# Second product of a feed-forward block in three 256-column matmuls, with its weights rounded at new homes

## The chip, the cores and the metric

The kernel runs on one NeuronCore of a Trainium2 chip. The metric is the time of one execution on the device in microseconds (us), as the median of several runs.

## What is computed

Attention through packed queries, a top-1 mixture of experts, and a feed-forward block follow each other. The change lies almost wholly in the last, `_moe2_ref`. The tensors that matter there are x [4608, 512], w_in [512, 2048] and w_out [2048, 512].

```python
def reference(**kwargs):
    ...
    attn_out = _attn_ref(**attn_kwargs)
    B, H, S, D = attn_out.shape
    x = np.ascontiguousarray(attn_out.transpose(0, 2, 1, 3)).reshape(B * S, H * D)
    x = _moe_ref(x=x, **moe_kwargs)
    return _moe2_ref(x=x, **moe2_kwargs)

def _moe2_ref(x, w_in, w_out) -> np.ndarray:
    h = x @ w_in
    g = h * (1.0 / (1.0 + np.exp(-h)))
    return (g @ w_out).astype(np.float32)
```

## The kernel before

The program has four stages: attention, experts, the feed-forward block's first product (x times W_in, with the activation) and its second (times W_out). Every float32 operand of TensorE is held as two parts: a high part, rounded by ScalarE (`ACT.copy` into an fp32r tile), and a low part, the rest, subtracted by VectorE. A product of two numbers is high x high, high x low and low x high. `tt` (line 849) is the helper behind every addition and subtraction of the feed-forward block, on VectorE or GpSimd, so its line stands in nearly all their rows.

Both products use a scheme of seven block products in place of eight: operands are cut in four quarters (A11, A12, A21, A22 and B11 to B22), sums and differences of quarters are made (S1 to S4, T1 to T4), and the table `terms` pairs them as products 1 to 7. Their results are combined when they are drained from PSUM.

**First product.** It runs in groups `group(z, g)`: z is a sweep over tokens (z = 0 to 3 hold 512 columns, z = 4 holds 256), g one of eight slices of W_in. One group has seven products `Pm`, each of six matmuls; the seventh (`last`) is issued behind the first product of the group after it. `order` is the list of groups behind the eight of z=0; its index is called i, and group 28 in what follows is the group with i = 28. Side work (rounding operands, loading) is queued with `later` and issued by `hook` in four places of a group, as far as a budget of nanoseconds reaches; `flush` issues all that is left. The results are stored in DRAM as c_d[z][0..4]: c11, c12, c21, c22, and for all z but 0 the sum E1 in [4] and a difference in place of c21. z=1 and z=3 share the operand tile X0; z=4 uses tiles `e` (both halves of `sums.ab`). W_in slices sit in four tiles TT[0..3] and are reloaded from t_d with `t_load`.

**Second product.** It runs over 18 units (four per z, two for z=4), each with seven products in `order3`, 126 in all. `split(s)` makes the high and low parts of product s in one of four slots (1024 columns each), `product(s)` runs over the eight slices of W_out, `drain(s)` takes PSUM out, `load_unit` loads the four quarters of a unit (512 KB each) from c_d, and `early_sums` either loads E1 or, where it was not stored, makes it. For each slice there are two matmuls: the high part against 512 columns (high and low W_out side by side), and the low part against 256, summed into the second half of the same PSUM bank:

```python
PE.matmul(out=o, lhsT=h[:, g], rhs=x, start=first and g == 0, stop=False, skip_group_check=True)
PE.matmul(out=o[:, 256:512], lhsT=l[:, g], rhs=x[:, 0:256], start=False, stop=g == 5, skip_group_check=True)
```

So each PSUM result is two half sums of 256 columns. Drains take 512 columns, and GpSimd adds the halves (`both`) before a write to the output.

**W_out.** Its slices are rounded while the first product runs. T1 to T4 of W_out are made in the expert stage by GpSimd (`conv`) and stored in u_d. Slices 5 to 7 go through `corner_steps` into small tiles, from there to v_d in DRAM, and come back with `slice_load` into TT[1..3]. Slice 0 gets homes of its own. Slices 1 to 4 are loaded in seven pieces of four slices into staging tiles (`staged`) and rounded into X0 (`build4`), four pieces at the end of the first product and three beside the first products of the second.

**Order and queues.** Each engine runs its instructions in program order, and the DMAs that an engine issues start in that order too, each behind its waits. Nearly all DMAs are issued by SyncE (SP).

## Time and profile before

| What | Value |
| --- | --- |
| Median of 3 runs | 1289.51 us (1285.29 to 1294.49) |
| The profiled execution, its own time | 1287.26 us |
| Its span, first to last instruction | 1285.4 us |
| Mean granted TensorE clock | 0.985 of full speed |
| TensorE busy | 1201.5 us, 93% |
| VectorE, ScalarE, GpSimd busy | 68%, 42%, 17% |
| First product of the feed-forward block | about 530 to 899 us |
| Second product | 899 to 1285 us |

Busy time is the union of an engine's instructions. Matmuls overlap in the pipeline, so the pace of TensorE is read from the distance between starts and not from the length of one. A time in brackets behind a row is how long the engine sat idle before it, with the one that released it. PEclk is the mean clock that TensorE was granted in a stretch, as a share of 2.4 GHz.

### The profile page before, as it was taken

The numbers are of one execution on the slowest core, as the hardware profiler recorded it, in microseconds if no ns is written. First come the engines' busy times: TensorE is split into PE (matmuls) and PEld (weight loads), VectorE is DVE, ScalarE is ACT, GpSimd is POOL, SyncE is SP. The second block draws the span as 40 slices with busy tenths as digits, with TensorE's granted clock in tenths as the row PEclk, the third lists the DMA queues.
The fourth block names the chain that finished last, engine by engine and source line by source line (L and its number), as shares of the span: only waits on it lengthen the run. The fifth ranks groups of instructions, "written<-read, shape, count | busy, mean of one in ns | idle before, by whom it ended". The sixth has DMA issues, their size and how long they took to land.

```text
span 1285.4 us, 23420 instructions
## 1 busy us (share of the span) xinstructions
PE 1201.5 (93%) x9008; PEld 1040.1 (81%) x9009; DVE 878.3 (68%) x1468; ACT 534.9 (42%) x901; POOL 214.1 (17%) x273
## 2 busy tenths in 40 slices
PE   6898989999999989999999999997878999999998
PEld 4677678999999989878788878776767888888886
DVE  2566657688887784786756667556756777767765
ACT  3666652332243224464444445334423433443342
POOL 3233210113212230100000000000112322323322
PEclk9999999999999999999999999999988999999999
DMA  6898738679877864675864554998744466475561
GB/s 193 247 264 223 238 100 295 218 234 334 275 257 265 279 215 139 201 228 207 335 224 174 193 171 160 377 364 268 239 119 132 125 173 172 132 189 145 151 186 44
DMA packets 260454, 272.67 MB, mean 212 GB/s; under 512 B 35305, under 2 KB 203497, under 8 KB 259057
## 3 DMA queue, kind: packets, MB, share of 16 engines
q1 hardware_dynamic: 253808, 266.40, 65.3%
q10 hardware_dynamic: 6528, 4.72, 1.2%
q8 instruction: 72, 1.18, 0.4%
q14 instruction: 46, 0.37, 0.1%
HBM read 171.59 MB, written 99.48 MB: 211 GB/s over the span
## 4 chain that ended last, share of the span: by engine, by line
PE 44%; DVE 8%; DMA 6%; issue 3%; ACT 2%; SPq 0%; DVEq 0%; POOLq 0%; POOL 0%; ACTq 0%
PE p L1129 17%; PE p L1130 8%; PE p L856 5%; PE p L858 5%; PE p L857 5%; DVE x L849 4%; DMA c_d<-x 1%; DMA x<-u_d 1%; DMA v_d<-e 1%; DVE raw L849 1%; DVE e L849 1%; PE ps L605 1%; PE ps L603 1%; PE ps L604 1%; DMA raww1c<-c_d 1%
## 5 line engine op out<-in xcount | busy, mean ns | idle before, releaser
L849 POOL TENSOR_TENSOR raw<-x 128x256 f32<-128x256 f32 x72 | 100.9, 1402 | 650.1 <-DMA rawe<-c_d 387.9
L849 DVE TENSOR_TENSOR x<-p,x 128x512 f32<-128x512 f32 (+1 forms) x170 | 109.4, 653 | 52.3 <-PE p L858 41.6
L889 ACT ACTIVATE x<-x 128x512 f32<-128x512 f32 (+1 forms) x113 | 67.3, 600 | 131.4 <-DVE x L849 126.2
L1129 PE MATMUL p<-x,e 128*128 128x512 f32 x315 | 118.2, 402 | 0.0
L605 PE MATMUL ps<-hkm,w2s 128*128 128x288 f32 x384 | 113.7, 296 | 2.8 <-DVE w2s L576 2.8
L603 PE MATMUL ps<-hkm,w2s 128*128 128x288 f32 x384 | 114.6, 298 | 1.3 <-DVE yb L614 1.3
L604 PE MATMUL ps<-hqm,w2s 128*128 128x288 f32 x320 | 94.2, 294 | 0.0
L1130 PE MATMUL p<-x,x 128*128 128x256 f32 x320 | 90.4, 282 | 0.0
L603 PEld LDWEIGHTS ps<-hkm,w2s 128*128 128x128 f32 x384 | 72.1, 188 | 7.7 <-DVE hqm L538 3.4
L605 PEld LDWEIGHTS ps<-hkm,w2s 128*128 128x128 f32 x384 | 72.0, 188 | 4.0 <-DVE w2s L576 4.0
L849 DVE TENSOR_TENSOR x<-p,y 128x512 f32<-128x512 f32 (+1 forms) x75 | 49.6, 662 | 36.9 <-PE p L858 26.2
L529 PE MATMUL ps<-at,mh 128*128 128x288 f32 x224 | 66.9, 299 | 7.0 <-PEq L694 4.5
L1129 PEld LDWEIGHTS p<-x,e 128*128 128x128 f32 x315 | 59.9, 190 | 14.9
L531 PE MATMUL ps<-at,mh 128*128 128x288 f32 x224 | 66.9, 298 | 0.0
L530 PE MATMUL ps<-at,mh 128*128 128x288 f32 x224 | 66.8, 298 | 0.0
L534 ACT ACTIVATE hkm<-ps 128x576 fp32r<-128x576 f32 x42 | 27.1, 650 | 85.8 <-PE ps L531 85.8
L575 ACT CAST w2s<-w2c 128x1024 fp32r<-128x1024 f32 x32 | 33.7, 1054 | 67.2 <-PE ps L604 36.6
L1130 PEld LDWEIGHTS p<-x,x 128*128 128x128 f32 x320 | 61.0, 191 | 0.0
L1129 PE MATMUL p<-x,x 128*128 128x512 f32 x160 | 60.5, 404 | 0.0
L604 PEld LDWEIGHTS ps<-hqm,w2s 128*128 128x128 f32 x320 | 60.0, 188 | 0.0
L1129 PE MATMUL p<-x,at 128*128 128x512 f32 x155 | 58.6, 405 | 0.0
L604 PE MATMUL ps<-hvm,w2s 128*128 128x288 f32 x192 | 56.6, 295 | 0.0
(409 smaller groups left out, 3547.4 us busy)
## 6 DMA issues: line engine op xcount, KB each, us to landing
c_d<-x SPq DMA_DIRECT2D x152, 256.0 KB, 2.4
raww1c<-c_d SPq DMA_DIRECT2D x36, 512.0 KB, 7.0
rawe<-c_d SPq DMA_DIRECT2D x36, 512.0 KB, 6.9
w1c<-in_moe_w_dram SPq DMA_DIRECT2D x32, 512.0 KB, 6.5
w2c<-in_moe_w_dram SPq DMA_DIRECT2D x32, 512.0 KB, 6.2
y_d<-yb SPq DMA_DIRECT2D x36, 288.0 KB, 4.8
raw<-y_d SPq DMA_DIRECT2D x36, 256.0 KB, 4.6
vm<-in_v_dram SPq DMA_DIRECT2D x8, 1024.0 KB, 10.7
```

The source lines that it names most:

```text
L529: PE.matmul(out=a[:, i, 0:H2], lhsT=mh[0][:, t, f], rhs=at[0][:, t, n], start=t == 0, stop=False)
L530: PE.matmul(out=a[:, i, 0:H2], lhsT=mh[0][:, t, f], rhs=at[1][:, t, n], start=False, stop=False)
L531: PE.matmul(out=a[:, i, 0:H2], lhsT=mh[1][:, t, f], rhs=at[0][:, t, n], start=False, stop=t == 1)
L603: PE.matmul(out=a[:, i, 0:H2], lhsT=h[:, k, :], rhs=hT(0, k, n), start=k == 0, stop=False)
L604: PE.matmul(out=a[:, i, 0:H2], lhsT=h[:, k, :], rhs=hT(1, k, n), start=False, stop=False)
L605: PE.matmul(out=a[:, i, 0:H2], lhsT=l[:, k, :], rhs=hT(0, k, n), start=False, stop=k == 7)
L849: eng.tensor_tensor(out=o, in0=x, in1=y, op=op)
L856: PE.matmul(out=o, lhsT=h, rhs=a[0][k][:, 0:n], start=start and k == 0, stop=False, skip_group_check=True)
L857: PE.matmul(out=o, lhsT=h, rhs=a[1][k][:, 0:n], start=False, stop=False, skip_group_check=True)
L889: ACT.activation(out=y, in_=x, func=ACTF.Silu)
L1129: PE.matmul(out=o, lhsT=h[:, g], rhs=x, start=first and g == 0, stop=False, skip_group_check=True)
L1130: PE.matmul(out=o[:, 256:512], lhsT=l[:, g], rhs=x[:, 0:256], start=False, stop=g == 5, skip_group_check=True)
```

## The change

The second product uses three matmuls of 256 columns per slice, all into one half bank: high x high, high x low, low x high. The half sums and GpSimd's additions go, and drains take 256 columns. A split is issued behind the drain two products before it, no longer ahead of it. W_out's T1 to T4 are made by VectorE in the feed-forward block (`out_sums`), stored in u_d (`u_store`) for six slices and used at once for slices 0 and 5. Slices 1 to 4 are loaded raw into X0 by GpSimd's queue (`x_load`) once the z=3 sweep is over, into the place of their own low parts, and rounded there (`x_build`). Slices 6 and 7 are loaded and rounded in TT[2] and TT[3] in the same way (`t_raw`, `t_build`); v_d goes. `t_load` moves to GpSimd's queue. The four products that begin unit 0 run over six slices first, and over slices 6 and 7 later. The first sweep's groups from i = 16 on stand in another order: four z=4 groups (28 to 31) now end it. Units run z = 1, 2, 0, 3, 4, and E1 is stored for z=1 and z=2 only (`FIVE`); for the others VectorE makes it in the second product.

```diff
-        if 7 < i < 16 or i >= 24:
+        if 7 < i < 16:
...
-                SP.dma_start(out=u_d[i - 8 if i < 16 else i - 16][:, 512 * n:512 * n + 512], in_=four[n])
+                SP.dma_start(out=u_d[i - 8][:, 512 * n:512 * n + 512], in_=four[n])
...
+    FIVE = (1, 2)
...
-                if not z:
+                if z not in FIVE:
                     store(2, c21)
                     return lambda: None
...
     def t_load(g, x):
         held[g] = x
-        SP.dma_start(out=TT[x][:, 0:3584].bitcast(F32), in_=t_d[g].bitcast(F32))
+        POOL.dma_start(out=TT[x][:, 0:3584].bitcast(F32), in_=t_d[g].bitcast(F32))
...
     def o_load(g):
-        o, p = room(), room()
-        SP.dma_start(out=o[:, 0:256], in_=w[16 + g, :, 0:256])
-        SP.dma_start(out=p, in_=w[24 + g])
-        x4_load(8 + g)
-        ow[g] = o, p
+        ow[g] = raw(w[16 + g]), raw(w[24 + g])
+
+    def out_sums(g, t=None):
+
+        o, p = ow[g]
+        b11, b12, b21, b22 = o[:, 0:256], o[:, 256:512], p[:, 0:256], p[:, 256:512]
+        t1, t2, t3, t4 = t or (b11, b22, b12, b21)
+        return [(425, lambda q=q, x=x, y=y: tt(DVE, q, x, y, ALU.subtract)) for q, x, y in ((t1, b12, b11), (t3, b22, b12), (t2, b22, t1), (t4, b21, t2))]
+
+    def u_store(g):
+        o, p = ow[g]
+        for n, x in enumerate((o[:, 0:256], p[:, 256:512], o[:, 256:512], p[:, 0:256])):
+            SP.dma_start(out=u_d[8 + g][:, 256 * n:256 * n + 256], in_=x)
...
-    units = [(z, r) for z in range(NP2) for r in range(4)] + [(NP2, r) for r in range(2)]
+    units = [(z, r) for z in (1, 2, 0, 3) for r in range(4)] + [(NP2, r) for r in range(2)]
...
     order3 = (1, 7, 6, 2, 5, 3, 4)
+    order0 = (1, 7, 6, 3, 2, 5, 4)
...
     def begin(i):
         if i == 0:
-            slots.append((half(b, 3), one.tile([128, 1024], F32R, name="x6", tag="x6")))
+            x = one.tile([128, 2048], F32R, name="x5", tag="x5")
+            slots.append((half(x, 0), half(x, 1)))
         else:
-            x = one.tile([128, 2048], F32R, name="x5", tag="x5")
-            slots.extend([(half(x, 0), half(x, 1)), (half(b, 0), half(b, 1)), at])
+            slots.extend([(half(X2, 0), half(X2, 1)), (half(b, 0), half(b, 1)), (half(X2, 2), half(b, 2))])
...
     def split(s):
         u, i = seq[s]
         c11, c12, c21, c22 = raws[u % 2]
-        src = {1: c11, 7: c21, 6: c11, 2: c12, 5: E1, 3: c12, 4: c22}[i]
-        h, l = slots[s % R]
-        ACT.copy(out=h, in_=src)
-        tt(DVE, l, src, h.bitcast(F32), ALU.subtract)
-        if i == 1:
-            tt(DVE, c11, E1, c11, ALU.subtract)
-        elif i == 2:
-            tt(DVE, c12, c12, c11, ALU.subtract)
-        elif i == 5 and 0 < u < len(units) - 1:
-            early_sums(u + 1)
+        src = {1: c11, 7: c21, 6: c11, 2: c12, 5: E1, 3: S4, 4: c22}[i]
+
+        def hi():
+            ACT.copy(out=slots[s % R][0], in_=src)
+
+        def lo():
+            h, l = slots[s % R]
+            tt(DVE, l, src, h.bitcast(F32), ALU.subtract)
+            if i == 1:
+                tt(DVE, c11, E1, c11, ALU.subtract)
+            elif i == 6:
+                tt(DVE, S4, c12, c11, ALU.subtract)
+            elif i == 5 and u < len(units) - 1:
+                early_sums(u + 1)
+        return hi, lo
 
     def early_sums(u):
-        if units[u][0]:
+        if units[u][0] in FIVE:
             load_unit(u, (4,))
             return
         c11, c12, c21, c22 = raws[u % 2]
         tt(DVE, E1, c21, c22)
         tt(DVE, c21, c11, c21, ALU.subtract)
...
-    def product(s, gs=(0, 1, 2, 3, 4, 6, 7, 5)):
+    def product(s, gs, start=True, stop=True):
         u, i = seq[s]
         w = terms[i][1]
         h, l = [eight(x) for x in slots[s % R]]
-        o = banks[u % 2][{1: 0, 2: 0, 6: 1, 5: 1, 7: 2, 4: 2, 3: 3}[i]]
-        first = i in (1, 6, 7, 3)
+        o = banks[u % 2][{1: 0, 2: 0, 6: 1, 5: 1, 7: 2, 4: 2, 3: 3}[i]][:, 0:256]
+        first = start and i in (1, 6, 7, 3)
         for g in gs:
             x = WO[g][w]
-            PE.matmul(out=o, lhsT=h[:, g], rhs=x, start=first and g == 0, stop=False, skip_group_check=True)
-            PE.matmul(out=o[:, 256:512], lhsT=l[:, g], rhs=x[:, 0:256], start=False, stop=g == 5, skip_group_check=True)
-
-    tn = [0]
+            PE.matmul(out=o, lhsT=h[:, g], rhs=x[:, 0:256], start=first and g == gs[0], stop=False, skip_group_check=True)
+            PE.matmul(out=o, lhsT=h[:, g], rhs=x[:, 256:512], start=False, stop=False, skip_group_check=True)
+            PE.matmul(out=o, lhsT=l[:, g], rhs=x[:, 0:256], start=False, stop=stop and g == gs[-1], skip_group_check=True)
...
+        a, b, c, d = [x[:, 0:256] for x in banks[u % 2]]
+        n = slice(0, 256)
         if i == 1:
-            ACT.copy(out=p1, in_=a)
-            outs[u] = {}
+            ACT.copy(out=p1[:, n], in_=a)
+            outs[u] = [room(), room()]
         elif i == 6:
-            tt(DVE, u2, b, p1)
+            tt(DVE, u2[:, n], b, p1[:, n])
         elif i == 2:
-            x = t()
-            ACT.copy(out=x, in_=a)
-            outs[u][0] = room()
-            both(outs[u][0][:, 0:256], x)
+            ACT.copy(out=outs[u][0][:, 0:256], in_=a)
         elif i == 5:
-            x = t()
-            tt(DVE, v, b, p1)
-            tt(DVE, x, c, v)
-            outs[u][1] = room()
-            both(outs[u][1][:, 256:512], x)
-        elif i == 3:
-            x = t()
-            tt(DVE, x, d, v)
-            both(outs[u][0][:, 256:512], x)
+            tt(DVE, v[:, n], b, p1[:, n])
+            tt(DVE, outs[u][1][:, 256:512], c, v[:, n])
+        if i == (3 if u else 5):
+            tt(DVE, outs[u][0][:, 256:512], d, v[:, n])
             write(z, r, 0, outs[u][0])
-        elif i == 4:
-            x = t()
-            tt(DVE, x, c, u2)
-            both(outs[u][1][:, 0:256], x)
+        if i == 4:
+            tt(DVE, outs[u][1][:, 0:256], c, u2[:, n])
             write(z, r, 1, outs[u][1])
...
-    def build4(x, src, eng, cast=None):
...
+    def put(d, src, w=None):
+
+        return (lambda: ACT.copy(out=d[:, :, 0:256], in_=src),
+                lambda: tt(DVE, d[:, :, 256:512], src, d[:, :, 0:256].bitcast(F32), ALU.subtract))
+
+    ahead = []
+
+    def chain(*pairs):
+
+        def f(hi, lo):
+            if hi:
+                hi()
+            if ahead:
+                ahead.pop()()
+            if lo:
+                ahead.append(lo)
+        return [(1230, lambda hi=hi, lo=lo: f(hi, lo)) for hi, lo in pairs]
...
+    def corner(g, place):
...
+        return chain(*[put(two(d), x) for d, x in zip(place, src)], (None, None))
+
+    place0 = (mh[1][:, 1024:1536], mh[0][:, 0:1024], mh[0][:, 1024:2048], mh[1][:, 0:1024])
+    place5 = (mh[1][:, 1536:2048], at[0], at[1], half(b, 3))
+
+    def x_load(x):
         i = 512 * names.index(x)
-        put(XX[:, :, i:i + 256], XX[:, :, i + 256:i + 512], src.bitcast(F32).rearrange("p (g n) -> p g n", g=4), eng, cast)
...
-    def staged(x, src):
-        SP.dma_start(out=src.rearrange("p (g n) -> p g n", g=4).bitcast(F32), in_=w_out(x, slice(1, 5)))
-        stage[x] = src
...
-    def slice_load(n, part=None):
-        for a, b in {None: ((0, 3584),), 0: ((0, 512), (2560, 3072)), 1: ((2048, 2560), (512, 1024)), 2: ((1024, 2048), (3072, 3584))}[part]:
-            SP.dma_start(out=TT[1 + n][:, a:b].bitcast(F32), in_=v_d[n][:, a:b].bitcast(F32))
...
+        POOL.dma_start(out=XX[:, :, i + 256:i + 512].bitcast(F32), in_=w_out(x, slice(1, 5)))
+
+    def x_build(x):
+        i = 512 * names.index(x)
+        d = XX[:, :, i:i + 512]
+        return put(d, d[:, :, 256:512].bitcast(F32))
+
+    def t_raw(g):
+        t = two(TT[g - 4])[:, :, 256:512].bitcast(F32)
+        SP.dma_start(out=t[:, 0], in_=w[16 + g, :, 0:256])
+        SP.dma_start(out=t[:, 1:3], in_=w[24 + g].rearrange("p (i n) -> p i n", n=256))
+        SP.dma_start(out=t[:, 3:7], in_=u_d[8 + g].rearrange("p (i n) -> p i n", n=256))
+
+    def t_build(g, a, b):
+        d = two(TT[g - 4])[:, a:b]
+        return put(d, d[:, :, 256:512].bitcast(F32))
...
-    next_t = {19: (4, 0), 20: (5, 1), 23: (6, 2), 24: (7, 3)}
-    b4 = lambda x: (1230, lambda: build4(x, stage[x], DVE))
+    order = [(1, 4), (1, 5), (1, 6), (1, 7), (2, 4), (2, 5), (2, 6), (2, 7), (1, 0), (1, 1), (1, 2), (1, 3), (2, 0), (2, 1), (2, 2), (2, 3),
+             (3, 0), (3, 1), (3, 2), (4, 0), (4, 1), (4, 2), (3, 3), (4, 3), (3, 4), (3, 5), (3, 6), (3, 7), (4, 4), (4, 6), (4, 7), (4, 5)]
+    need = {(2, 4): 2, (3, 0): 3, (4, 0): 4}
+    next_t = {19: (4, 0), 20: (5, 1), 21: (6, 2), 23: (7, 3)}
+    wsum = {8: 1, 9: 2, 19: 3, 21: 4, 22: 6, 24: 7, 25: 0, 26: 5}
+    order2 = ("B11", "T3", "T2", "B22", "B21", "T1", "T4")
...
-        if i in (19, 21, 23, 25):
-            n = (i - 19) // 2
+        if i in wsum:
+            x = wsum[i]
+            o_load(x)
+            if x in (0, 5):
+                later(now + 4, *out_sums(x, tmp), *corner(x, place5 if x else place0))
+            else:
+                later(now + 4, *out_sums(x), (0, lambda x=x: u_store(x)))
+        if i == 28:
             flush()
...
-            for x, y in (("B11", at[0]), ("T3", at[1]), ("T2", half(b, 3)), ("B21", x4)):
-                staged(x, y)
-        if i == 28:
+            load_unit(0, (4,))
+            later(now + 1, (0, small))
+        if i == 29:
+            for x in order2:
+                x_load(x)
+        if i == 30:
             raws[0] = quarters("w1c")
             load_unit(0)
-        if i == 29:
-            later(now + 1, (0, small))
-            later(now + 1, b4("B11"), b4("B21"), b4("T3"))
-        if i == 30:
-            later(now, (0, lambda: slice_load(1)))
-            later(now, b4("T2"), (0, lambda: early_sums(0)), (0, lambda: split(0)))
+            later(now + 1, *chain(*[x_build(x) for x in order2[0:3]]))
         if i == 31:
-            later(now + 1, (0, lambda: slice_load(2)), (0, lambda: begin(1)), (0, lambda: split(1)))
+            t_raw(6)
+            later(now, *chain(*[x_build(x) for x in order2[3:5]], split(0), *[x_build(x) for x in order2[5:7]], (None, None)))
         group(z, g)
         if i - 1 in next_t:
             t_load(*next_t[i - 1])
 
+    S4 = one.tile([128, 1024], F32, name="x6", tag="x6")
     flush()
...
-    pend.pop()()()()
-    slice_load(0, 0)
-    slice_load(0, 1)
...
-    last = {"T1": (1, co[0]), "B22": (2, co[1]), "T4": (3, [half(b, 2)[:, 0:512], half(b, 2)[:, 512:1024]])}
...
+    pend.pop()()()
     raws[1] = quarters("e0")
+    begin(1)
+    t_raw(7)
+    load_unit(1)
+    early = (0, 5, 1, 2, 3, 4)
+    product(0, early, True, False)
+    for s in range(1, R):
+        for f in (*chain(split(s), t_build(6, 2 * s - 1, 2 * s + 1)), *(chain((None, None)) if s == R - 1 else ())):
+            f[1]()
+        product(s, early, True, False)
+    for f in chain(t_build(6, 0, 1), *[t_build(7, a, a + 2) for a in (1, 3, 5)], t_build(7, 0, 1), (None, None)):
+        f[1]()
     for s in range(len(seq)):
         u, i = seq[s]
-        if i == (1 if u else 6) and u + 1 < len(units):
+        if u and i == 1 and u + 1 < len(units):
             load_unit(u + 1)
-        if s == 5:
-            early_sums(1)
-        if s + L < len(seq):
-            split(s + L)
-        for x, (n, t) in last.items():
-            if n == s:
-                for j in range(2):
-                    o = 512 * names.index(x)
-                    d = XX[:, 2 * j:2 * j + 2, o:o + 512]
-                    put(d[:, :, 0:256], d[:, :, 256:512], two(t[j]).bitcast(F32), DVE)
-        if s < 2:
-            product(s, (0, 1, 2, 3, 4, 6, 7))
-            if s:
-                for x in range(2):
-                    product(x, (5,))
-                    drain(x)
+        if s < R:
+            product(s, (6, 7), False)
         else:
-            product(s)
-            drain(s)
+            product(s, range(G))
+        drain(s)
+        if R <= s + L < len(seq):
+            for f in split(s + L):
+                f()
```

## Rows read from the trace of the kernel before

**Rows 1.** Page, busy time: engine, us (share of span), instructions.

```profile
PE 1201.5 (93%) x9008; PEld 1040.1 (81%) x9009; DVE 878.3 (68%) x1468; ACT 534.9 (42%) x901; POOL 214.1 (17%) x273
```

**Rows 2.** Table by stretches: length, busy (instructions) of each engine, PEclk, DMA share, GB/s.

```profile
835.00:860.00 25.00, 23.16 (x124) 19.62 (x123) 12.92 (x26) 8.36 (x18) 0.00 (x0) 1.00 1.01 373
882.00:899.00 17.00, 11.13 (x73) 10.52 (x74) 11.97 (x19) 6.33 (x13) 0.00 (x0) 0.90 0.62 202
930.00:945.00 15.00, 7.56 (x44) 6.33 (x42) 7.98 (x8) 4.84 (x6) 1.97 (x2) 0.81 0.63 176
945.00:972.00 27.00, 22.77 (x114) 19.46 (x115) 17.55 (x17) 8.11 (x9) 6.59 (x4) 0.88 0.35 97
```

**Rows 3.** TensorE's waits, 882 to 980: total us, times, longest.

```profile
PE p L1129 <- DVE y L849: 11.7, 2, 7.4
PE p L856 <- DVE raw L849: 4.4, 2, 4.0
PE p L1129 <- DMA t<-v_d: 3.5, 1, 3.5
```

**Rows 4.** TensorE's waits, 787 to 882.

```profile
PE p L856 <- DVE y L849: 4.5, 3, 1.7
PE p L856 <- ACT y L928: 3.0, 1, 3.0
```

**Rows 5.** TensorE's timeline, first matmuls of products: start, us, line, tiles, size.

```profile
898.88 0.39 PE L1129 MATMUL p<-mh,e 128*128 128x512 f32 x1
...
909.85 0.39 PE L1129 MATMUL p<-mh,e 128*128 128x512 f32 x1
...
912.63 0.39 PE L1129 MATMUL p<-mh,at 128*128 128x512 f32 x1
...
955.60 0.40 PE L1129 MATMUL p<-mh,e 128*128 128x512 f32 x1
...
1002.18 0.40 PE L1129 MATMUL p<-mh,e 128*128 128x512 f32 x1
...
1273.54 0.40 PE L1129 MATMUL p<-mh,e 128*128 128x512 f32 x1
```

**Rows 6.** TensorE's timeline in a z=4 group, ten steps apart.

```profile
850.15 0.28 PE L857 MATMUL p<-e,ta 128*128 128x256 f32 x1
...
851.35 0.28 PE L858 MATMUL p<-e,ta 128*128 128x256 f32 x1
```

**Rows 7.** Page, costliest groups: weight loads; busy us, mean ns of one.

```profile
L1130 PEld LDWEIGHTS p<-x,x 128*128 128x128 f32 x320 | 61.0, 191 | 0.0
```

**Rows 8.** VectorE's timeline: a drain, an early sum, a low part.

```profile
885.01 0.42 DVE L849 TENSOR_TENSOR x<-x,y 128x256 f32<-128x256 f32 x1
...
967.66 1.22 DVE L849 TENSOR_TENSOR x<-rawe 128x1024 f32<-128x1024 f32 x1 [3.85 <-DMA rawe<-c_d]
...
968.92 1.63 DVE L849 TENSOR_TENSOR rawe<-rawe 128x1024 f32<-128x1024 f32 x1
...
970.48 0.68 DVE L849 TENSOR_TENSOR y<-p,y 128x512 f32<-128x512 f32 x1
...
1105.71 1.23 DVE L849 TENSOR_TENSOR e<-rawe,e 128x1024 fp32r<-128x1024 f32 x1 [2.28 <-ACT e L1104]
```

**Rows 9.** VectorE's and GpSimd's timelines at the end.

```profile
1279.46 0.69 DVE L849 TENSOR_TENSOR x<-p,y 128x512 f32<-128x512 f32 x1 [2.12 <-PE p L1130]
...
1280.23 0.72 POOL L849 TENSOR_TENSOR raw<-x 128x256 f32<-128x256 f32 x1 [2.07 <-DVE x L849]
```

**Rows 10.** SyncE's timeline: output writes, a unit's loads.

```profile
956.80 2.07 SPq L1175 DMA_DIRECT2D out_dram<-raw  x2
959.00 4.65 SPq L1077 DMA_DIRECT2D rawe<-c_d  x4
```

**Rows 11.** ScalarE's timeline: a copy of 256 columns, a cast of 1024.

```profile
881.90 0.35 ACT L928 COPY y<-p 128x256 f32<-128x256 f32 x1
...
1104.62 1.05 ACT L1104 CAST e<-rawe 128x1024 fp32r<-128x1024 f32 x1
```

More of the change, by code (lines that the diff above doesn't have):

```diff
@@ L210, in build @@
         with ExitStack() as s1:
-            ffn(tc, s1, sums, y_d, wf_d, t_d, c_d, u_d, v_d, out)
+            ffn(tc, s1, sums, y_d, wf_d, t_d, c_d, u_d, out)
 class Early:
@@ L819, in experts, with ffn @@
                 conv_store(x)
-def ffn(tc, st, sums, y_d, wf_d, t_d, c_d, u_d, v_d, out):
+def ffn(tc, st, sums, y_d, wf_d, t_d, c_d, u_d, out):
     nc = tc.nc
@@ L1210, in ffn @@
     cut = lambda x, o: x[:, o:o + 512]
-    two = lambda x: x.rearrange("p (i n) -> p i n", i=2)
+    two = lambda x: x.rearrange("p (i n) -> p i n", n=512)
     names = ("B11", "B21", "B22", "T1", "T2", "T3", "T4")
     WO = [{x: cut(mh[i // 4], 512 * (i % 4)) for i, x in enumerate(("B21", "B22", "T1", "T2", "T3", "T4", "B11"))}]
-    WO += [{m: cut(x, 512 * i) for i, m in enumerate(names)} for x in (*[X0[:, 3584 * i:3584 * i + 3584] for i in range(4)], *TT[1:])]
+    WO += [{m: cut(X0, 3584 * g + 512 * i) for i, m in enumerate(names)} for g in range(4)]
@@ L1215, in ffn @@
+    five5 = [cut(mh[1], 1536), cut(at[0], 0), cut(at[0], 512), cut(at[1], 0), cut(at[1], 512), cut(half(b, 3), 0), cut(half(b, 3), 512)]
+    WO += [dict(zip(names, five5))]
+    WO += [{m: cut(x, 512 * i) for i, m in enumerate(names)} for x in TT[2:]]
     XX = X0.rearrange("p (g n) -> p g n", g=4)
-    order2 = ("B11", "T3", "T2", "B21", "T1", "B22", "T4")
-    def corner_steps(g, place, eng=DVE):
-        o, p = ow.pop(g)
-        def f(i, src):
-            d, done = place(i)
-            if i:
-                put(two(d)[:, :, 0:256], two(d)[:, :, 256:512], two(src), eng)
-            else:
-                put(d[:, 0:256], d[:, 256:512], src, eng)
-            if done:
-                done(d)
-        return [(1500 if i else 800, lambda i=i, x=x: f(i, x)) for i, x in enumerate((o[:, 0:256], p, x4[:, 0:512], x4[:, 512:1024]))]
@@ L1231, in slice0 @@
-    def slice0(i):
-        return ((mh[1][:, 1024:1536], mh[0][:, 0:1024], mh[0][:, 1024:2048], mh[1][:, 0:1024])[i], None)
-    ring = [*at, half(b, 3)]
-    def slices(n):
-        def place(i):
-            t = ring.pop(0)
-            ring.append(t)
-            a, b = ((0, 512), (512, 1536), (1536, 2560), (2560, 3584))[i]
-            return t[:, 0:b - a], lambda d: SP.dma_start(out=v_d[n][:, a:b].bitcast(F32), in_=d.bitcast(F32))
-        return place
-    def build4(x, src, eng, cast=None):
-        i = 512 * names.index(x)
-        put(XX[:, :, i:i + 256], XX[:, :, i + 256:i + 512], src.bitcast(F32).rearrange("p (g n) -> p g n", g=4), eng, cast)
```

34 lines of the change are left out of this document (7 added, 27 removed).

## The prediction

> **What bounds the kernel now.** I read the page first, for the share of each engine: TensorE is busy 1201.5 us of a span of 1285.4 [rows 1], so time can only come from its idle stretches, from its clock, or from its pace. Then the table by stretches: from 882 to 899 TensorE works 11.1 of 17 us at a mean granted clock of 0.90; from 930 to 945 it works 7.6 of 15; from 945 to 972 its clock averages 0.88 [rows 2]. This is the passage from the first product of the feed-forward part to the second, and the list of waits names what ended the idle time: a VectorE drain of the second product (11.7 us in two waits, the longer 7.4), a VectorE operation of the last z=4 groups (4.4), a load of v_d (3.5) [rows 3]. The stretch before it, 787 to 882, has shorter waits of the same kind between groups of z=4 [rows 4].
>
> The start times of products then size it. Product to product in the quiet stretch is (1273.54 - 1002.18)/96 = 2.827 us; nothing there waits. At that pace the 126 products need 356.2 us. They run from 898.88 to 1273.54 + 2 x 2.827 = 1279.19, which is 380.3: **24.1 us lost**, all of it in units 0 and 1 [rows 5]. The z=4 groups from 882 lose 17 - 11.1 = 5.9 us of idle time and about 17 x 0.10 = 1.7 us of clock, 7.6 together [rows 2]. So the passage costs 31.7 us over a full TensorE, and the groups before it 4.5 + 3.0 = 7.5 [rows 4]. These 39 us are what the reordering can win; the rest of the span is TensorE's pace.
>
> **The change part by part. Three matmuls of 256 columns** (for one of 512 and one of 256) stream the same 768 columns, at 2.4 GHz 320 ns. A pair takes 2.827/8 = 353.3 ns. The nearest row for the new form is a z=4 group, also 256 columns with a weight load each: ten steps from 850.15 to 851.35, 120.0 ns each [rows 6]. Three make 360.0, so 6.7 ns more per slice, x 8 x 126 = **+6.7 us**. Lower bound: pairs ran at (912.63 - 909.85)/8 = 347.5 in one product [rows 5], and triples like that would give -5.9 us. Upper bound: the overhead of a steady pair, (353.3 - 320)/2 = 16.7 ns per matmul, paid three times, is 370 ns, +16.8 us. I take the row of the same form.
>
> A rule speaks against this part. The rows show weight loads hidden: a load lasts 0.19 us [rows 7] and the matmuls that have one each still start every 0.12. The Trainium skill (TensorE: Matmul & The Clock Gate, Part 3, The mechanism) says a weight load overlaps running matmuls only when it targets another row group. Full 128-row weights would then never overlap, and the third load per slice, at the page's 107 ns, would be an estimated 108 us. Here the trace disagrees with it.
>
> **No half sums.** The 72 additions on GpSimd go, and VectorE's drains shrink from 0.69 to 0.42 us [rows 8]. Both are hidden under TensorE in the quiet stretch, where VectorE is not late. They show at the end of the program: the last drain is 0.69 us and the GpSimd addition ends 0.80 us after it [rows 9]; now it is 0.42 and the write follows at once: 0.27 + 0.80 = **-1.1 us**. VectorE gains besides: a 1024-column subtraction beside GpSimd took 1.63 us, alone 1.22 [rows 8].
>
> **The passage.** Count from the start of group 28, the first of the last four z=4 groups. At full pace a z=4 group is 42 x 0.12 = 5.04 us, so four and the last product of the previous sweep end near 21, and the first four products of unit 0 would end at 21 + 4 x 2.88 = 32.5. What can be late:
> - The loads into X0 start when the last z=3 product has read it, near 2.1. They are 3.67 MB, with unit 0's E1 and the stores of c_d some 5.2 MB; at the 373 GB/s that a full stretch moved [rows 2] that is 14 us, the last near 17, B11 near 6. The builds start in group 30, near 12, in load order, so they are covered by 4 to 6 us. GpSimd's queue, which issues them and the t_d loads, has no other work there. Its issue cost no row shows: between nothing and 3 us per load the cover holds; past that each microsecond per load costs up to 5.
> - SyncE loses these issues, and four loads held it 4.65 us [rows 10]. By the Trainium skill (DMA: Bandwidth & Descriptors, Issuing engines are not separate DMA queues) the other queue buys issue time and no bandwidth; on this reckoning the 14 us stand either way. Unit 0's four quarters go out behind the stores of group 29, near 12, and land between 18 and 26; queued behind them are the stores of group 30 and T6's raw slices (near 28), and behind group 31's last store T7's (near 32).
> - VectorE is late next. From 12 it has seven builds and the low part and difference of the first operand, 9 x 1.22, the low part of the second, 1.22, and some nine drains x 0.42: 16 us, so the second product starts near 28, while the first six slices of product 0 end at 22 + 6 x 0.36 = 24. Then T6 pieces, the S4 difference and two low parts put product 3 near 35 to 37, the builds of T7 end near 38.4, four products of two slices take 4 x 0.72, and the fifth waits about 1 us for its operand, split behind the drain of the third: 42.4 against 32.5, **10 us lost**. Cold clock after the gaps of 3 us is in it, as part of the waiting.
> - The four groups themselves: 28 and 29 carry no builds and one sum and one difference less than before; I give them and 30, 31 3 us.
>
> So 13 us in place of 31.7, **-18.7**. Bounds: -28 (the splits and builds all covered but for the last drain) and 0 (the same queueing as now, with T7 as the late load).
>
> **The groups before.** v_d's writes go, z=3 and z=4 lose a sum, a difference and a store per group, while eight slices add four differences of 0.42 each on VectorE (13.4 us over eight groups; VectorE was busy 12.9 of 25 us there [rows 2]). Corner work stays for two slices of four. I let half of the 7.5 remain: **-3.7**, bounds -7 and +4 (three z=4 groups now stand in a row). In the expert stage 32 GpSimd differences and 16 stores go, beside a TensorE that is full: 0, bounds -1 and 0.
>
> **The quiet stretch.** Two things can be late. (a) Units of z=0, 3 and 4 now come from u=8 on, and ten times VectorE makes E1 and c21 itself, when the next unit's quarters have landed. Today that sum waited: load issued at 959.00, sum at 967.66, 8.7 us [rows 8, 10], because the load stood behind the writes at 956.80, which wait for GpSimd; and behind the sum stood the drain (970.48) that the next product needed. Counted from the unit's start at 955.60 [rows 5] the sum came at +12.1. After the change the write is ready at +0.8 to 1.1, takes 1.04, and the third quarter lands near 2.1 + 8.7 = 10.8 to 11.7; the drain stands ahead of the sum. Then 2 x 1.22 and the next low part 1.22 end at 14.4 to 15.3, against 14.4 + 0.24 when product 3 wants it. That is 0 to 0.7 us x 10: **+3**, bounds 0 and +10. (b) A split is now issued after the drain of the product two before it. For products 1 and 2 ScalarE copies (0.35), casts (1.05) [rows 11], VectorE subtracts (1.23) [rows 8]; with 0.2 from product end to the copy that is 2.83 against 2.88 + 0.24: covered by 0.3. If the handovers are half a microsecond longer, 36 x 0.2 = +7; I take 0.
>
> **Sum** against the profiled run's own 1287.3 (span 1285.4, 1.9 around it; the median of the three runs is 1289.5): 6.7 - 1.1 - 18.7 - 3.7 + 3 = -13.8, **1273.5 us**.
>
> **The rivals.** (1) *The passage is limited by its transfers and in-order queues as before.* ScalarE and VectorE take X0's builds, unit 0 and T7 in order, and one late load holds all behind it. For it: the waits of rows 3 are all of this kind, and my reckoning has T7 late already. Against: v_d's 11 MB of writes and reads leave the same stretch. With 13 us more lost: 1286. (2) *Nearly all of the passage is covered,* the builds running into the z=4 groups and the products of six slices bridging the rest: 9 us better, 1264. Against it stands VectorE's 16 us. (3) *The early sums stall the quiet stretch: slower.* If the third quarter lands at +15 instead of +11, VectorE stands still in each of ten units, and each costs what the second of the two drain waits did: 11.7 - 7.4 = 4.3 us, and by the clock of 0.88 over the 27 us that hold both some 1.6 each [rows 2, 3]. That is 10 x 6 = 60 in place of the 3 of the sum: 1331. It decides from a landing later than +11; the order of drain and sum and the earlier write speak against it. (4) *The third weight load shows in full:* up to 1008 x 0.19 = 190 us [rows 7], 1465; the steps of 0.12 in [rows 6] against it. It is what the page's rule above would do here. (5) *It does not do what it says,* the passage keeping its waits for another reason, is the end of (1), 1292.
>
> **How the numbers follow.** Forecast 0.50 (own range 1263 to 1283), (1) with (5) 0.24, (2) 0.17, (3) 0.07, (4) 0.02. The range takes the forecast's bounds, all of (1) and half of (2), and leaves out (3), (4) and the better half of (2): 1258 to 1292. One per cent, about what a measurement of this kernel can tell from no change, is below 1276.6. Faster: 0.33 of the forecast's 0.50, all of (2), 0.04 of (1): 0.54, and I round to 0.56; slower, (3), (4) and a little of (1): 0.10; the rest 0.34.
>
> **What would show it.** In the profile after: three matmuls per slice at 0.120 us and products at 2.88 us (2.78 to 2.96 would be my bounds); no GpSimd additions there; the first product of unit 0 near the end of group 31 with a gap of about 3 us behind its first six slices, then one before T7's slices; no wait longer than 1 us after u=1, with short ones on VectorE's low part of product 3 from u=7 on. Wrong would be: waits on X0's loads (GpSimd's issue), waits in each unit from u=7 on (rival 3), or a product pace beyond 2.96.

## The result, and the profile after

The changed kernel runs in **1268.41 us** (median of four runs, 1267.54 to 1269.88) against 1287.82 for the kernel before on the same chip: a ratio of 0.9843, 95% interval 0.9802 to 0.9883. The forecast was 1273.5, in a range from 1258 to 1292 that holds the measured time. Run once more, beside experiments 5 to 7, the changed kernel gave 1267.28 (0.9842). Its profiled execution took 1268.04, with a span of 1265.6, 19.8 less than before.

The page of the changed kernel answers to [rows 1]: TensorE does the same work in a shorter span, and GpSimd has lost 122 us.

```profile
PE 1202.6 (95%) x10016; PEld 1090.8 (86%) x10017; DVE 853.7 (67%) x1477; ACT 522.4 (41%) x898; POOL 92.6 (7%) x180
```

The table by stretches of the changed kernel, for [rows 2] (length, busy us of PE, PEld, DVE, ACT, POOL, then PEclk, DMA share, GB/s):

```profile
804.00:820.00 16.00, 8.49 (x32) 6.65 (x31) 3.64 (x9) 1.90 (x4) 0.53 (x1) 0.81 0.98 385
820.00:870.00 50.00, 50.00 (x254) 42.68 (x254) 28.33 (x54) 20.09 (x38) 5.39 (x8) 0.99 0.63 218
870.00:882.00 12.00, 12.00 (x102) 12.00 (x101) 6.98 (x15) 6.63 (x14) 0.37 (x1) 1.00 1.02 333
882.00:890.00 8.00, 5.89 (x42) 5.28 (x41) 7.33 (x10) 5.65 (x10) 0.00 (x0) 0.94 0.97 264
890.00:900.00 10.00, 6.94 (x36) 6.54 (x36) 8.03 (x10) 5.46 (x8) 0.00 (x0) 0.71 1.04 325
900.00:920.00 20.00, 18.09 (x147) 17.51 (x146) 13.31 (x18) 8.55 (x14) 0.00 (x0) 1.00 0.54 155
920.00:1000.00 80.00, 80.00 (x669) 80.00 (x668) 49.90 (x56) 29.51 (x36) 0.00 (x0) 1.00 0.57 157
1000.00:1260.00 260.00, 260.00 (x2169) 260.00 (x2169) 184.84 (x199) 94.12 (x115) 0.00 (x0) 1.00 0.47 127
```

TensorE is full and at full clock from 820 to 882 and from 920 to the end. Two holes are left: 804 to 820, which the kernel before did not have in this form, and 882 to 920, the passage. Its waits from 870 to 1000 answer to [rows 3]. There is none after 1000.

```profile
PE p L1142 <- ACT x L1113: 2.3, 1, 2.3
PE p L1144 <- DVE x L847: 1.9, 3, 0.8
PE p L854 <- DVE y L847: 1.3, 1, 1.3
PE p L1142 <- DVE raw L847: 1.1, 1, 1.1
```

The one wait of TensorE from 780 to 870, in the first product (L854 to L856), answers to [rows 4]:

```profile
PE p L854 <- DVE y L847: 7.5, 1, 7.5
```

TensorE's timeline, for [rows 5, 6]: the first matmul of group 28, the first two of product 0, the first of the second product (both over six slices), the first of the fifth, then the first matmuls of two steady products 2.88 apart, and the last matmul of all. Each slice is L1142, L1143, L1144.

```profile
864.33 0.28 PE L854 MATMUL p<-e,ta 128*128 128x256 f32 x1
...
888.29 0.28 PE L1142 MATMUL p<-mh,x 128*128 128x256 f32 x1
888.41 0.28 PE L1143 MATMUL p<-mh,x 128*128 128x256 f32 x1
...
895.06 0.38 PE L1142 MATMUL p<-mh,x 128*128 128x256 f32 x1 [2.30 <-ACT x L1113]
...
907.16 0.28 PE L1142 MATMUL p<-mh,x 128*128 128x256 f32 x1
...
923.87 0.28 PE L1142 MATMUL p<-mh,x 128*128 128x256 f32 x1
...
926.75 0.28 PE L1142 MATMUL p<-mh,e 128*128 128x256 f32 x1
...
1260.71 0.28 PE L1144 MATMUL p<-t,x 128*128 128x256 f32 x1
```

Products run from 888.29 to 1260.83. The places of the 19.8 us, from these starts and [rows 5]: the feed-forward block starts at 522.83 (before 523.18), -0.35; its first product takes 365.5 (before 375.7), -10.2; its 126 products take 372.5 (380.3), -7.8; from the last product to the end of the span it is 4.8 (6.2), -1.4.

### The profile page after: what moved, and what is told of

The parts are those of the page before. It is cut to its first block, busy times and chain, and to the rows that moved or that the text cites. A ratio compares the mean times of both kernels' runs of the same rounds, so it can differ in the third digit from the quotient of the medians.

```text
span 1265.6 us, 25188 instructions
## 1 busy us (share of the span) xinstructions
PE 1202.6 (95%) x10016; PEld 1090.8 (86%) x10017; DVE 853.7 (67%) x1477; ACT 522.4 (41%) x898; POOL 92.6 (7%) x180
## 3 DMA queue, kind: packets, MB, share of 16 engines
q0 software_dynamic: 1584, 11.01, 2.5%
## 4 chain that ended last, share of the span: by engine, by line
PE 50%; DVE 5%; DMA 4%; issue 2%; ACT 1%; SPq 0%; DVEq 0%; ACTq 0%
PE p L1144 9%; PE p L1143 9%; PE p L1142 9%; PE p L854 6%; PE p L855 6%; PE p L856 6%; DVE x L847 2%; DMA c_d<-x 2%; DMA raw<-wf_d 1%; DVE raw L847 1%; PE ps L604 1%; PE ps L602 1%; PE ps L603 1%; PE ps L528 0%; PE ps L530 0%
## 5 line engine op out<-in xcount | busy, mean ns | idle before, releaser
L847 DVE TENSOR_TENSOR x<-p,x 128x512 f32<-128x512 f32 (+1 forms) x132 | 83.4, 643 | 55.8 <-PE p L856 42.7
L1142 PE MATMUL p<-x,x 128*128 128x256 f32 x380 | 108.5, 286 | 0.0
L1143 PE MATMUL p<-x,x 128*128 128x256 f32 x380 | 108.4, 285 | 0.0
L1142 PEld LDWEIGHTS p<-x,x 128*128 128x128 f32 x380 | 74.0, 195 | 0.0
L1143 PEld LDWEIGHTS p<-x,x 128*128 128x128 f32 x380 | 73.9, 195 | 0.0
L1144 PE MATMUL p<-x,x 128*128 128x256 f32 x256 | 73.2, 286 | 0.0
L1144 PE MATMUL p<-x,e 128*128 128x256 f32 x248 | 70.2, 283 | 0.0
L847 DVE TENSOR_TENSOR x<-p,y 128x512 f32<-128x512 f32 (+1 forms) x57 | 33.2, 582 | 39.1 <-PE p L856 31.7
L847 DVE TENSOR_TENSOR x<-x,x 128x512 f32<-128x512 f32 (+2 forms) x58 | 49.5, 853 | 14.4 <-ACT x L1113 11.5
L1152 ACT COPY y<-p 128x256 f32<-128x256 f32 x18 | 6.7, 372 | 126.4 <-PE p L1144 126.4
```

Source lines behind the costliest of these rows:

```text
L847: eng.tensor_tensor(out=o, in0=x, in1=y, op=op)
L1142: PE.matmul(out=o, lhsT=h[:, g], rhs=x[:, 0:256], start=first and g == gs[0], stop=False, skip_group_check=True)
L1143: PE.matmul(out=o, lhsT=h[:, g], rhs=x[:, 256:512], start=False, stop=False, skip_group_check=True)
L1144: PE.matmul(out=o, lhsT=l[:, g], rhs=x[:, 0:256], start=False, stop=stop and g == gs[-1], skip_group_check=True)
```

## The experiments

All are edits of the changed kernel, but for the fifth, which is one of the kernel before. Each ratio is to the kernel before on the same chip (1287.50 for the first to fourth, 1290.07 for the fifth to seventh and the second run of the changed kernel, 1286.97 for the rest). The stages ahead of the feed-forward block end between 519.4 and 528.6 us in the profiled executions, with edits that don't reach them; so lengths are compared from that block's first matmul. In the expectations, e1, e2 and e9 are experiments 1, 2 and 6.

**1. The pairs back.** What is the three-matmul form worth when the rest of the change stands?

```diff
-            PE.matmul(out=o, lhsT=h[:, g], rhs=x[:, 0:256], start=first and g == gs[0], stop=False, skip_group_check=True)
-            PE.matmul(out=o, lhsT=h[:, g], rhs=x[:, 256:512], start=False, stop=False, skip_group_check=True)
-            PE.matmul(out=o, lhsT=l[:, g], rhs=x[:, 0:256], start=False, stop=stop and g == gs[-1], skip_group_check=True)
+            PE.matmul(out=o, lhsT=h[:, g], rhs=x, start=first and g == gs[0], stop=False, skip_group_check=True)
+            PE.matmul(out=o[:, 256:512], lhsT=l[:, g], rhs=x[:, 0:256], start=False, stop=stop and g == gs[-1], skip_group_check=True)
...
+            tt(POOL, o, x[:, 0:256], x[:, 256:512])
```

The drains take 512 columns again, as before the change.

> The changed kernel with the second product's old form put back: a matmul of 512 and one of 256 columns, half sums, GpSimd's additions; all else as changed. Theory (the form costs 6.7 us of pace and gives back 1.1 to 1.4 at the end): products at 2.827 instead of 2.880 us, about 5.5 us less than the changed kernel, 1263. Rival (the additions hold VectorE back beside them, 1.63 for 1.22 us, and the ten early sums of the late units then stall TensorE): 1268 to 1275, with waits on VectorE from u=7 on.

Measured: **1300.66** (1295.8 to 1306.6), ratio 1.0098 [1.0068, 1.0128]. Both expectations missed, by 25 us and more. Its list of TensorE's waits, 1000 to 1300 (us, times, longest), shows ten waits in the units whose sums VectorE makes:

```profile
PE p L1144 <- DVE x L847: 11.1, 5, 2.4
PE p L1144 <- DVE e L847: 9.7, 5, 2.7
```

One of them followed back. GpSimd, SyncE, VectorE and TensorE in the timeline of this kernel:

```profile
1088.25 1.65 POOL L847 TENSOR_TENSOR raw<-x 128x256 f32<-128x256 f32 x1 [1.76 <-DVE x L847]
...
1090.37 5.09 SPq L1084 DMA_DIRECT2D raww1c<-c_d  x4
...
1099.90 1.23 DVE L847 TENSOR_TENSOR x<-raww1c 128x1024 f32<-128x1024 f32 x1 [2.55 <-DMA raww1c<-c_d]
...
1103.58 0.39 PE L1144 MATMUL p<-mh,x 128*128 128x256 f32 x1 [2.21 <-DVE x L847]
```

GpSimd's addition ends at 1089.90, the write that wants it has to leave before the next unit's loads, these go out at 1090.37, and the early sum waits for them at 1099.90, with the low part for TensorE behind it. From 1000.29 to 1291.09 the 723 distances between slices exceed the steady 0.3533 by 35.4 us: 23.4 in the ten slices that hold the waits, and some 12 in slices behind eight of them, 0.64 us apart at half the clock. That is 3.5 us a unit. Less the 5 us that the pairs' faster pace saves in these slices, and with 1.1 more at the tail, it covers the 32 us that this kernel lies behind the changed one.

**2. The t_d loads on SyncE.**

```diff
-        POOL.dma_start(out=TT[x][:, 0:3584].bitcast(F32), in_=t_d[g].bitcast(F32))
+        SP.dma_start(out=TT[x][:, 0:3584].bitcast(F32), in_=t_d[g].bitcast(F32))
```

> The changed kernel with the loads of t_d back on SyncE's queue. Theory (the wait of 7.5 us at 808 to 816 is made by three of these loads, 1.8 MB each, that GpSimd's free queue issues at 794, 799 and 805 and that fill the transfers): on SyncE they stand behind the stores and spread; the wait falls below 2 us and the time to about 1260. Rival (stores, sums' loads and SyncE's own issue time fill that stretch anyway): the wait stays at 5 to 10 us, time 1267 to 1272.

Measured: **1257.63** (1254.76 to 1264.05), ratio 0.9759 [0.9711, 0.9807]: the lowest median of all runs. The wait of 7.5 us is gone (no wait from 780 to 870), and the first product takes 355.6 us instead of 365.5. (Its profiled execution, 1264.05, is the longest of the six; the block starts 5.8 us later in it.) First GpSimd's, then SyncE's and VectorE's timeline of the changed kernel, where the wait arises:

```profile
794.11 0.71 POOL L1036 DMA_DIRECT2D ta<-t_d  x1 [264.54 <-PE p L856]
799.15 0.55 POOL L1036 DMA_DIRECT2D x<-t_d  x1 [4.33 <-PE p L856]
804.84 0.53 POOL L1036 DMA_DIRECT2D t<-t_d  x1 [5.14 <-PE p L856]
...
797.46 1.55 SPq L898 DMA_DIRECT2D c_d<-x  x3
...
811.68 0.43 DVE L847 TENSOR_TENSOR x<-p,x 128x256 f32<-128x256 f32 x1 [7.52 <-DMA c_d<-x]
815.07 0.43 DVE L847 TENSOR_TENSOR raw<-raw 128x256 f32<-128x256 f32 x1 [2.97 <-DMA raw<-wf_d]
815.41 0.69 DVE L847 TENSOR_TENSOR y<-p,y 128x512 f32<-128x512 f32 x1
```

And SyncE's timeline of the edited kernel with its table for the same stretch below:

```profile
804.62 0.40 SPq L1036 DMA_DIRECT2D ta<-t_d  x1
...
809.50 0.44 SPq L1036 DMA_DIRECT2D x<-t_d  x1
...
821.51 0.41 SPq L1036 DMA_DIRECT2D t<-t_d  x1
```

```profile
804.00:820.00 16.00, 15.90 (x94) 13.81 (x93) 7.32 (x15) 4.84 (x11) 0.00 (x0) 1.00 0.97 351
```

From GpSimd's otherwise empty queue three loads of 1.84 MB (128 x 3584 x 4 bytes) leave within 10.7 us. VectorE stands for 7.52 us until a store lands and its tile is free, then 2.97 for a slice of W_out, and the drain that TensorE wants (815.41) is behind both. That store had left SyncE before the second of the three loads: issued at 797.46, it landed at 811.59, 14.1 us later, where the median of this line's stores on the page is 2.3; the load issued at 799.15 landed at 809.32. So the loads overtook not only what SyncE had yet to issue, but also what it had issued. How the changed kernel's transfer engines were shared from 795 to 814.5 (packets, MB, share of the engines; q0 is GpSimd's queue, which moved 11.01 MB in this kernel and 3.67 in experiment 2, q1 SyncE's):

```profile
q0 software_dynamic: 432, 5.51, 73.7%
q1 hardware_dynamic: 1531, 1.66, 23.9%
```

On SyncE the same loads take their turn among the stores. Counted from the block's first matmul (528.63 there, 522.83 in the changed kernel) the first two leave some 5 us later and the third 11. The transfer engines are as full in either kernel: 0.98 and 0.97 from 804 to 820, and in the edited kernel 1.04 with 15.90 of 16 us of TensorE from 810 to 826, the stretch as far from the block's start. What differs is which bytes go first. The Trainium skill (DMA: Bandwidth & Descriptors, Issuing engines are not separate DMA queues) says that issuing from several engines saves issue time and nothing else; on bandwidth the trace agrees (385 GB/s with two queues from 804 to 820, 351 to 380 with one), but the other queue also changed which bytes go first, and that cost about 10 us.

**3. The split back ahead of the product two before it.**

```diff
+        if R <= s + L < len(seq):
+            for f in split(s + L):
+                f()
         if s < R:
             product(s, (6, 7), False)
         else:
             product(s, range(G))
         drain(s)
-        if R <= s + L < len(seq):
-            for f in split(s + L):
-                f()
```

> The changed kernel with each split issued ahead of the product two before it, as before the change. Theory (what keeps the early sums harmless is that the drain stands ahead of them): VectorE waits for the quarters ahead of a drain, and each of ten units from u=7 on loses about 2 us, 1285 to 1292, with waits on u2's drain. Rival (the quarters land in time since the write is no longer late, and the order does not matter): at most 3 us more, 1268 to 1271.

Measured: **1285.85** (1281.69 to 1289.85), ratio 0.9979 [0.9949, 1.0009], 17 to 19 us behind the changed kernel. The main entry of TensorE's waits from 1000 to 1280, and VectorE's timeline in one unit:

```profile
PE p L1142 <- DVE y L847: 11.5, 9, 2.2
```

```profile
1068.16 1.23 DVE L847 TENSOR_TENSOR x<-rawe 128x1024 f32<-128x1024 f32 x1 [3.46 <-DMA rawe<-c_d]
1069.42 1.23 DVE L847 TENSOR_TENSOR rawe<-rawe 128x1024 f32<-128x1024 f32 x1
1070.56 0.42 DVE L847 TENSOR_TENSOR y<-p,y 128x256 f32<-128x256 f32 x1
```

The early sum stands 3.46 us for its load with a drain behind it. In the changed kernel the drain is ahead and the sum comes later, with no wait, as VectorE's timeline there shows:

```profile
1068.07 0.42 DVE L847 TENSOR_TENSOR y<-p,y 128x256 f32<-128x256 f32 x1 [0.91 <-PE p L1144]
...
1069.67 1.23 DVE L847 TENSOR_TENSOR x<-rawe 128x1024 f32<-128x1024 f32 x1
```

**4. No products over six slices first.**

```diff
-    product(0, early, True, False)
...
-        product(s, early, True, False)
...
-            product(s, (6, 7), False)
+            product(s, early + (6, 7))
```

> The changed kernel without the six slices first: the first four products run over all eight slices in order, after the same splits and builds. Theory (TensorE would stand until slices 6 and 7 are built): three products of six slices, 3 x 2.16 = 6.5 us, are no longer done in the wait: 1275, with one wait of 5 us or more before slice 6 of product 0. Rival (the passage is set by VectorE's and ScalarE's queues behind it, the products only fill holes): 2 us or less, 1268 to 1270.

Measured: **1278.05** (1272.27 to 1279.41), ratio 0.9912 [0.9882, 0.9943]: some 10 us lost, with a mean granted clock of 0.79 from 880 to 920. TensorE's waits from 870 to 1000 have a new head, the builds of the last slices of W_out:

```profile
PE p L1142 <- ACT t L1218: 8.4, 1, 8.4
```

**5. Three matmuls alone, in the kernel before** (product and drains as in the change, everything else as before).

```diff
-            PE.matmul(out=o, lhsT=h[:, g], rhs=x, start=first and g == 0, stop=False, skip_group_check=True)
-            PE.matmul(out=o[:, 256:512], lhsT=l[:, g], rhs=x[:, 0:256], start=False, stop=g == 5, skip_group_check=True)
+            PE.matmul(out=o, lhsT=h[:, g], rhs=x[:, 0:256], start=first and g == 0, stop=False, skip_group_check=True)
+            PE.matmul(out=o, lhsT=h[:, g], rhs=x[:, 256:512], start=False, stop=False, skip_group_check=True)
+            PE.matmul(out=o, lhsT=l[:, g], rhs=x[:, 0:256], start=False, stop=g == 5, skip_group_check=True)
```

> The kernel before with one part of the change alone: three matmuls of 256 columns, no half sums, drains of 256 columns; order, loads and W_out as before. Theory (the form costs 6.7 us of pace but takes GpSimd's addition out of the way from a drain to the write and to the loads behind it): the drain waits of units 1 and 2 (11.7 us and slower clock) shrink to about a half, 1282 to 1287. Rival (the form costs its pace and gives back the end alone): those waits stay, 1291 to 1294.

Measured: **1284.10** (1278.65 to 1287.28), ratio 0.9962 [0.9934, 0.9991]. The two drain waits of [rows 3], 11.7 us, fell to 3.9 in its list from 880 to 1000, which pays for the slower pace:

```profile
PE p L1129 <- DVE y L849: 3.9, 2, 3.2
```

Whether the shorter drains did that, or the missing additions that had held the writes back, this run does not part.

**6. The pairs with the unit's loads issued earlier,** to test the cause found in experiment 1: a unit's loads leave before the writes that wait for GpSimd.

```diff
-        if u and i == 1 and u + 1 < len(units):
-            load_unit(u + 1)
+        if s % 7 == 5 and u + 2 < len(units):
+            load_unit(u + 2)
```

> Run e1 (the changed kernel with pairs and half sums) with a unit's four loads issued two products earlier, ahead of the writes that wait for GpSimd. Theory (e1 lost its time because the quarters land late, VectorE itself having room): no wait on a low part from u=7 on, pace 2.827, 1260 to 1264. Rival (drains of 512 columns and the slower sums beside GpSimd make VectorE late whatever the loads do): waits of 1 to 2 us remain in ten units, 1280 or more.

Measured: **1268.16** (1262.69 to 1269.27), ratio 0.9839 [0.9796, 0.9883]. The 32 us of experiment 1 are gone, so the cause, loads that leave late, was the right one. But it lies between the two expectations and gains nothing over the changed kernel: in its waits from 1000 to 1266 ten small ones are left,

```profile
PE p L1144 <- DVE x L847: 1.6, 5, 0.3
PE p L1144 <- DVE e L847: 1.4, 5, 0.3
```

and from product to product it takes (1257.08 - 1000.17)/89 = 2.887 us on average, against 2.88. So the pairs lose in steps of 0.1 to 0.6 us what their pace of 2.827 had won; the ten waits are 3.0 of the 5.3 us, the rest is not explained.

**7. Both: pairs, early loads, t_d on SyncE.**

> Run e9 with the loads of t_d on SyncE's queue as in e2. Theory (the two gains have different places and add): the time of e9 less 8 to 10 us, 1250 to 1256. Rival (they share transfers or queue time in the passage): less than 5 us below e9.

Measured: **1260.90** (1256.66 to 1264.17), ratio 0.9781 [0.9738, 0.9825]: 7.3 less than experiment 6, between the two expectations. The wait of 7.5 us is gone here too, with 1.3 left.

**8. X0's loads on SyncE.**

```diff
-        POOL.dma_start(out=XX[:, :, i + 256:i + 512].bitcast(F32), in_=w_out(x, slice(1, 5)))
+        SP.dma_start(out=XX[:, :, i + 256:i + 512].bitcast(F32), in_=w_out(x, slice(1, 5)))
```

> The changed kernel with X0's seven loads on SyncE's queue in place of GpSimd's. Theory (what the other queue buys is issue time: seven issues of 0.6 to 1.2 us stand ahead of group 29's stores and of unit 0's quarters): 3 to 8 us more, 1270 to 1276, with a longer wait at the first products. Rival (the transfers are the limit there and the queue does not matter): within 2 us of the changed kernel, 1266 to 1269.

Measured: **1270.36** (1265.53 to 1273.65), ratio 0.9861 [0.9822, 0.9900]: no different from the changed kernel within the intervals. By the medians GpSimd's queue is worth 2 to 3 us for these loads, which is not shown.

**9. Sums of five slices stored for z=3 too** (`FIVE = (1, 2, 3)`).

> The changed kernel with E1 and the difference stored for z=3 as well, so that two sums per group go back to the first product and four of the ten early sums leave the second. Theory (neither place is on the path: no wait in the quiet stretch after the change): 1266 to 1270. Rival (the first product's z=3 groups were late on VectorE): 3 us or more longer, with waits between 787 and 870.

Measured: **1272.23** (1270.46 to 1273.52), ratio 0.9876 [0.9828, 0.9924]. The intervals overlap; not settled. Its profiled span is 5.9 us longer (1271.5), but 3.8 of them lie ahead of the feed-forward block, which the edit does not reach, and as the theory has it no wait stands after 1000.

**10. The second and third t_d load placed one group later in the program, still on GpSimd.**

```diff
-    next_t = {19: (4, 0), 20: (5, 1), 21: (6, 2), 23: (7, 3)}
+    next_t = {19: (4, 0), 21: (5, 1), 22: (6, 2), 23: (7, 3)}
```

> The changed kernel with the second and third load of t_d issued one group later, still on GpSimd's queue. Theory (the burst of three loads makes the wait of 7.5 us near 810, not the queue that they stand in): wait below 3 us, 1258 to 1263, as in e2. Rival (GpSimd's queue itself, whose transfers go ahead of SyncE's, makes it): 5 us or more of the wait stay, 1265 to 1269.

Measured: **1268.96** (1264.38 to 1272.98), ratio 0.9856 [0.9815, 0.9897], and the wait stays at 7.4 us. GpSimd's timeline of this kernel shows why it tells nothing of the burst:

```profile
799.46 0.55 POOL L1036 DMA_DIRECT2D x<-t_d  x1 [4.33 <-PE p L856]
805.14 0.53 POOL L1036 DMA_DIRECT2D t<-t_d  x1 [5.14 <-PE p L856]
```

The loads leave when they left before. The queue holds nothing else, and each goes as soon as TensorE has released its buffer, wherever it stands in the program.

**11. Experiment 2 with the last product's drains ahead of the builds still queued** (`pend.pop()()()` ahead of `flush()`), for the 2.3 us wait of the second product for ScalarE's copy, 3.8 in the profiles of experiment 2 and of the changed kernel's second run.

> Run e2 (t_d on SyncE) with the last product of the first sweep and its drains issued ahead of the builds that are left over, no longer behind them. Theory (the second product of unit 0 waits for ScalarE, which stands at the last activation, which waits for VectorE behind two builds): that wait of 2.3 to 3.8 us falls below 1 us, 1254 to 1256 where e2 has 1257.6. Rival (VectorE's 16 us of work come before the second product in any order): no change.

Measured: **1260.12** (1258.74 to 1263.12), ratio 0.9793 [0.9756, 0.9830]. The wait is 3.8 us still: no effect. With experiment 2 this puts t_d on SyncE at 7 to 11 us.

**12. The changed kernel again,** beside experiments 5 to 7.

> The changed kernel once more, as the reference on this chip: 1267 to 1270.

Measured: **1267.28** (1263.96 to 1272.79), ratio 0.9842 [0.9798, 0.9886].

## Why the prediction was right

The likeliest case came true: faster by 1.6%, with the passage as the main source. The forecast was 5 us too high. By the number alone rival 2 (1264) lies as near; by its places the case is the forecast's, since the passage still loses 11.9 us, where I had 13 and rival 2 some 4. That the number came so near is in part luck: a wait of 7.5 us that I had not foreseen stood against a passage that gained more and early sums that cost less. Without it (experiment 2) the kernel runs at 1257.6, 16 us below the forecast. By places, against the profiled run: first product predicted -8.3 (-3.7 for the groups before and 7.6 - 3 for the last four), measured -10.2; the 126 products predicted 6.7 - 14.1 + 3 = -4.4, measured -7.8; tail predicted -1.1, measured -1.4; experts 0 and -0.35.

- **Three matmuls, +6.7: right.** Steps of 0.12 and products of 2.88 exactly, (2.88 - 2.827) x 126 = 6.7; rival 4 is out. The sentence of the Trainium skill (TensorE: Matmul & The Clock Gate, Part 3, The mechanism), by which weight loads overlap running matmuls only when the row group differs, is contradicted again: each slice has three loads, and 24 of them lie inside every product of 2.88. The same section also lets a load for the background weight buffer go ahead of running matmuls, and with that the steps agree.
- **The passage, -18.7: right in its course, -22.3 measured.** From 888.29 the products lose 372.5 - 126 x 2.88 = 9.7 us, where I had 10. Counted from the start of group 28 (864.33), the second product starts at +30.7, where I had 28, and the fifth at +42.8, where I had 42.4. The last z=4 groups are harder to compare, since [rows 2] undercount: adding up by how much the distances between matmul starts exceed the full pace, the stretch from 880 lost 10.1 us before and 2.2 after, where I had 7.6 and 3. Experiment 4 shows what the products over six slices give: 10 us.
- **The groups before, -3.7: right in sign, wrong in reason.** By the same count the stretch from 780 to 880 lost 12.3 us before and 9.9 after, so the gain was 2.4. The many short waits went, but one wait of 7.5 us with a granted clock of 0.81 took their place. The step that failed is that GpSimd's queue "has no other work there", by which I took the t_d loads on it to be free. An empty queue was the harm: its loads took three quarters of the transfer engines, and the stores and loads that VectorE needed landed late (experiment 2). Nearly all of those 9.9 us were to be had: by the same count experiment 2 loses 1 to 3 us there. That GpSimd's issue itself does not hold the X0 loads was right: seven issues of 0.75 us each.
- **The early sums, +3: the mechanism right, the size 0.** In one unit that starts at 1059.23 the loads left at 1060.27, the third quarter landed at 1068.99, +9.8 where I had +10.8 to 11.7, and the sum ran at 1069.67 without a wait. Rival 3 did not happen, and both things I named against it are what prevented it, as two experiments show: with the split ahead of the product it costs 17 to 19 us (experiment 3), with writes that wait for GpSimd 32 (experiment 1), at 3.5 us a unit where my price was 6.
- **No half sums, -1.1 at the tail and otherwise hidden: the tail right (-1.4), "hidden" wrong.** In the kernel before the form alone brought 6 us (1 to 8, experiment 5): with it the waits of [rows 3] shrank. In the changed kernel it is worth 32 (experiment 1), because ten units now make their sums on VectorE, behind loads that stood behind GpSimd. I named "the earlier write" against rival 3, but priced this part by itself at -1.1, without what the early sums owe to it; experiment 6 shows that earlier loads would have done as well.

What stays open: whether t_d's loads would harm less on GpSimd's queue if they were spread (experiment 10 did not spread them); the 2.3 to 3.8 us wait of the passage's second product, which experiment 11 did not move; and what the passage's gain beyond the 10 us of experiment 4 owes to each of the new group order, X0's raw loads and the end of v_d, which no run parts.

## What to carry to other kernels

A DMA moved to an engine with an empty queue leaves the moment its buffer is free, and its transfers can land ahead of what the busy queue has already issued: ask what they overtake, and keep bulk prefetch in the queue whose order paces it. Price the parts of a change together as well as each against the kernel before: a part that is free alone can be what lets another one run. When an operation that waits for a load shares an engine with a drain, put the drain first.

## What the runs showed of the hardware

Transfer engines at a share of 0.98 and 385 GB/s can be the sign of a stall and not of progress: in that stretch of the changed kernel TensorE worked 8.49 of 16 us, and at 0.97 and 351 GB/s in experiment 2 15.90. Two queues did not share the engines evenly there: 73.7% of their time went to GpSimd's three large loads, 23.9% to SyncE's stores and loads (experiment 2).

The clock answered to short waits. In TensorE's timeline of experiment 1, a wait of 1.97 us was followed by slices 0.64 us apart, which is 768 columns at 1.2 GHz (granted clock 0.50 from 1128.6 to 1131.9); a wait of 1.38 us in another unit was followed by the usual 0.35 (1.00 from 1150.1 to 1156):

```profile
1127.20 0.39 PE L1144 MATMUL p<-mh,e 128*128 128x256 f32 x1 [1.97 <-DVE e L847]
...
1129.09 0.63 PE L1143 MATMUL p<-at,x 128*128 128x512 f32 x1
...
1129.73 0.63 PE L1143 MATMUL p<-t,x 128*128 128x512 f32 x1
...
1150.10 0.38 PE L1144 MATMUL p<-mh,e 128*128 128x256 f32 x1 [1.38 <-DVE e L847]
...
1151.02 0.39 PE L1143 MATMUL p<-x,e 128*128 128x512 f32 x1
...
1151.37 0.39 PE L1143 MATMUL p<-x,e 128*128 128x512 f32 x1
```

Even so most of the price of such waits is the waits themselves (23.4 of 35.4 us).
